# A recurrence that feeds a routed MoE: due times of the static plan taken from a table

## The chip, the cores and the metric

The kernel runs on one core of a Trainium2 chip. The time is the device time of one execution in microseconds (us), a median over runs. The engines are named as the profile names them: PE (matrix unit; PEld its weight loads), DVE (vector), ACT (scalar), POOL (GpSimd), SP (the queue that issues most DMAs).

## The reference, cut to what matters

```python
# 4 sequences of 5056 tokens, 256 channels; 20224 tokens in all
sig = 1 / (1 + exp(-f_logit)); f = lower_bound + (1 - lower_bound) * sig
h[t] = f[:, t] * h[t-1] + (1 - f[:, t]) * x[:, t]     # along each sequence
expert = token_ids * 2654435761 % 8                   # one of 8 experts for each token
out[token] = relu(h[token] @ w1[expert]) @ w2[expert] # w1: 256 x 1024, w2: 1024 x 256
```

The multiplier is 1 modulo 8, so a token's expert is `id & 7`, and the kernel sorts the tokens by that.

## The kernel before, in words

**Stages.** The 5056 steps are cut into 24 blocks of 64, 128 or 256 steps (`TS`), all four sequences together; a block has two to eight *groups* of 128 tokens (158 in all). Blocks 0 to 6 bring the channels onto the partitions with PE transposes (tasks `trf`, `trx`, line 602), take the sigmoid on ACT (`sig`), the gate (`fg`), a product on DVE (`st`), the scan on DVE (`sc`), and go back through PE (`yt`) and a copy (`ye`). Blocks 7 to 23 use DVE's 32x32 transposes instead (`tf`, `tx`, line 783; `yt`, line 843), with the sigmoid of a whole half block on ACT ahead of them (`sig`, line 756). Loads (`ldf`, `ldx`) come from SP; a pool of three pairs of buffers (`XF`) holds them.

**Sort.** Each token's rank within its expert is counted in four ranges of groups (0 to 6, 6 to 46, 46 to 78, 78 to 158): one-hot and running sum (`ra`), PE (`rpe`), `rb`, `rc`, and a split of the rank into tile and row (`rd`). For groups from 46 on, the ids come by `tok` loads, and `ra9` extracts them. `zfd` is a one-element memset on DVE that follows the fill of a stretch of the sorted array `srt` with zeros. POOL then writes each group's rows of h to `srt` by an indirect DMA (`si`, line 537), 158 in all.

**Experts.** An expert's slots are 21 tiles of 128 rows; 168 tiles in all. A tile is read with a DMA transpose from SP (`rd`, line 935), multiplied by w1 (`up`, line 944), relu on ACT (`re`, line 953), multiplied by w2 (`dn`, line 962), copied for two tiles at a time (`oc`, line 970), and its rows go to `out` by an indirect DMA from POOL (`ro`, line 976), 168 in all. Windows say which blocks can reach which tile: tile j may be read when the scatters of block `last[j]` and all before it are out. Tables (`tb`, `tp`, `ta`) find the token of each slot, which `ro` needs. A flag (`flag`, `flagpe`, `flagc`) tells whether a token fell out of its window, for a fallback behind a branch at the end.

**Order.** Nothing is scheduled at run time: each engine works through one list in order. `Plan.order` makes the lists ahead of time. Each task has an engine, an assumed duration, dependencies, buffers and a number, its due time; among tasks that could start within a short look-ahead, the one with the lowest due time goes first. A weight has, besides, an earliest time (`rel`). Block k is due at 6 + 2.3 us for each group before it (`due`), its tables 25 later (`TABD`), its tiles 20 after its end (`OFF`), its rows 8 after its start. The plan's times shape the order only; on the chip engines wait on semaphores. A task at the head of a list that can't start holds back all behind it. On POOL, scatters `si`, rows `ro` and weights `w` share one list; on SP, loads and tile reads do.

Of the kernel before, what the change touches and what calls it, by code (L numbers as in the profile page):

```python
# [1 line left out]

# [6 lines left out]
FP32 = mybir.dt.float32  # L9
# [18 lines left out]
G0 = [sum(NGS[:k]) for k in range(NB)]
# [4 lines left out]
FILL = (9, 12)  # L33
XF = 3
OFF, TABD = 20.0, 25.0
W0, W1 = 8.0, 4.0


def sd(chunks):
# [3 lines left out]
def window(k):  # L43

    a, b = G0[k], G0[k] + NGS[k]
    if a >= MID:
        a, b = NG - b, NG - a
    lo = max(int((16 * a - Z * sd(a)) // P), 0) if a else 0
    hi = int((16 * b + Z * sd(b)) // P)
    return (lo, hi) if G0[k] < MID else (TPE - 1 - hi, TPE - 1 - lo)  # L50


class Task:
# [94 lines left out]
def kernel(  # L148
# [10 lines left out]
    nc = tc.nc  # L159
# [54 lines left out]
    diag = rp.tile([P, 4], FP32, name="diag")  # L214
    diag_i = rp.tile([P, 4], I32, name="diag_i")
    hand = rp.tile([P, 8], FP32, name="hand")
    handt = rp.tile([P, 8, 4], FP32, name="handt")
    row_id = rp.tile([P, NG], I32, name="row_id")
    row_t = rp.tile([P, NG], I32, name="row_t")
# [120 lines left out]
            nc.gpsimd.dma_start(lb_col[:], lower_bound.rearrange("(h p) -> p h", h=2))  # L340

    def load_lbc():
        with nc.allow_non_contiguous_dma(reason="256 values"):
            for b in range(B):
                nc.sync.dma_start(lb_c[32 * b:32 * b + 32, :], lower_bound.rearrange("(c j) -> j c", c=8))

    nz = (FILL[1] - FILL[0]) * D
    zero = rp.tile([P, nz], BF16, name="zero")
# [13 lines left out]
        nc.vector.tensor_scalar(c_col[:], lb_col[:], -1.0, 1.0, op0=ALU.mult, op1=ALU.add)  # L362

    def lbc_dve():
        nc.vector.tensor_scalar(c_c[:], lb_c[:], -1.0, 1.0, op0=ALU.mult, op1=ALU.add)

    lbl = add("lb", {"POOL": 0.9}, -101, load_lb, dma=0.8, lat=2.0)
    ip = add("ip", {"POOL": 4.0}, -100, init_pool)
    ip1 = add("ip1", {"POOL": 2.5}, -99, init_pool1)
    idv = add("idv", {"DVE": 0.2}, -100, init_dve)  # L370
    idv2 = add("idv2", {"DVE": 0.5}, -99, init_dve2, [ip])
    wm = add("wm0", {"DVE": 0.1}, -98, lambda: nc.vector.memset(wrm[:], 0.0))
    add("wm", {"ACT": 1.5}, -98, warm, [wm])
    zf = add("fill", {"SP": 0.5}, -5, fill, [ip1], dma=4.5, lat=2.0)
    ip2 = add("ip2", {"POOL": 4.0}, 0, init_pool2)
    ip3 = add("ip3", {"POOL": 2.0}, 60, init_pool3)
    idv3 = add("idv3", {"DVE": 1.2}, 12, init_dve3, [ip, ip2])
    idv4 = add("idv4", {"DVE": 0.8}, 30, init_dve4, [idv2, ip2])
    lbcl = add("lbcl", {"SP": 1.8}, 20, load_lbc, dma=0.5, lat=2.0)
    lbc = add("lbc", {"DVE": 0.1}, 40, lbc_dve, [lbcl])  # L380
    lbd = add("lbd", {"DVE": 0.1}, -95, lb_dve, [lbl])
    idl = {}
    for k in range(KS):
        idl[k] = add(f"ids{k}", {"ACT" if k < 4 else "POOL": 1.2 if TS[k] > 64 else 1.4},
                     k - 105 if k < 4 else k - 99.5, lambda k=k: load_ids(k), dma=0.6, lat=2.0)
    tokl = [add(f"tok{b}", {"SP": 0.45}, -30, lambda b=b: load_tok(b, 0), dma=0.4, lat=2.0) for b in range(B)]
    if NA % 32:
# [70 lines left out]
        nc.vector.tensor_copy(lo_h[:, a:b], r_i[:])  # L458

    ranked, split = {}, {}  # L460
    zfd = add("zfd", {"DVE": 0.1}, 5, filled, [zf])
    ras = {}
    r0a = add("ra9", {"DVE": 0.8}, 13, rank_0a, tokl + [idv])
    for ri, (a, b) in enumerate(RANGES):
        n = b - a
        pr = (-60, 1, 15, 29)[ri]
        r0 = r0a if a >= GA else add(
            f"ra{a}", {"DVE": 0.4}, pr, lambda a=a, b=b: rank_0(a, b), [idl[k] for k in range(KS) if a <= G0[k] < b]
        )
        ras[a] = add(f"ra{a}", {"DVE": 0.4 + n * 0.028}, pr, lambda a=a, b=b: rank_a(a, b), [r0, idv2, ip1])  # L470
    for ri, (a, b) in enumerate(RANGES):
        n = b - a
        pr = (-60, 1, 15, 29)[ri]
        need = [ras[p] for p, q in RANGES if (q <= b if a < MID else p >= a)]
        rbs = []
        for g in range(2):
            key = ("hp", ("rps", a, g))
            rpe = add(f"rpe{a}{g}", {"PE": 1.0 + n * 0.007}, pr, lambda a=a, b=b, g=g: rank_pe(a, b, g),
                      need + [idv], alloc=key)
            rbs.append(add(f"rb{a}{g}", {"DVE": 0.1 + n * 0.0042}, pr, lambda a=a, b=b, g=g: rank_b(a, b, g),  # L480
                           [rpe], use=[key]))
        rc = add(f"rc{a}", {"DVE": 0.35 + n * 0.013}, pr, lambda a=a, b=b: rank_c(a, b), rbs + ([zfd] if a >= GA else []))
        rd = add(f"rd{a}", {"DVE": 1.4}, 18 + 10 * ri, lambda a=a, b=b: rank_d(a, b), [rc])
        for k in range(NB):
            if a <= G0[k] < b:
                ranked[k], split[k] = rc, rd
# [27 lines left out]
        nc.vector.reduce_max(m[:], v[:], axis=mybir.AxisListType.X)  # L514
        nc.vector.tensor_copy(flag_i[:], m[:])

    mf = add("flag", {"DVE": 0.9}, 150, make_flag, list(set(ranked.values())) + [ip3])
    fp = add("flagpe", {"PE": 0.1}, 151, flag_pe, [mf], alloc=("op", "flag"))
    add("flagc", {"DVE": 0.5}, 152, flag_out, [fp], use=[("op", "flag")])

    weights = []
    for e in range(E):
# [5 lines left out]
                    nc.gpsimd.dma_start(w2_sb[e][:], moe_w2[e].rearrange("(k p) d -> p k d", p=P))  # L528
            weights.append(add(f"w{e}{v}", {"POOL": 0.85}, 5, wl, rel=W0 + W1 * (2 * e + v), dma=2.8, lat=2.0))

    due = {k: 6 + 2.3 * G0[k] for k in range(NB)}
    scat = {}

    prev_y, evs = {}, {}
# [9 lines left out]
    for k in range(KS):  # L544
# [36 lines left out]
        for u in range(nu):  # L581
# [11 lines left out]
            for h in range(2):  # L593
# [32 lines left out]
                def scan(un=un, h=h, bs=bs, k=k, tt=tt):  # L626
# [24 lines left out]
                        use=[ks, kx] + ([kv] if h else []), after=scs)  # L651
                f1 = not T["new", k]
                a = add(
                    f"sc{k}.{u}", {"DVE": nb * 0.06 + cols * 0.00229}, hp_, scan, [a],
                    alloc=ky if f1 else None, use=[ks, kv] + ([] if f1 else [ky]) + ([("y", k - 1)] if k else []),
                    after=scs + ([] if f1 else [T["new", k][0]]),
                )
# [203 lines left out]
    for k in range(NB):  # L861
        jlo, jhi = win[k]
        W = 8 * (jhi - jlo + 1)
        ng = NGS[k]

        def tb(c0, c1, k=k, jlo=jlo, W=W):
            if c0 == 0:
                T["tb", k] = (
                    mp.tile([P, NGM, P], BF16, name="A", bufs=1), mp.tile([P, NGM, 2, WMAX], BF16, name="BP", bufs=1)
                )  # L870
            A, BP = T["tb", k]
            n = c1 - c0
# [37 lines left out]
        pr = due[k] + TABD  # L910
        parts = []
        for c0 in range(0, ng, 4):
            c1 = min(c0 + 4, ng)
            parts.append(add(
                f"tb{k}", {"DVE": 0.4 + (c1 - c0) * (128 + 3 * W) / 960}, pr, lambda c0=c0, c1=c1, f=tb: f(c0, c1),
                [split[k], idv3, evs[k]] + parts[:1], alloc=None if parts else ("tb", k), use=[("tb", k)] if parts else [],
            ))
        b = add(f"tp{k}", {"PE": ng * (0.03 + 2 * W / 2400)}, pr, tpe, parts, alloc=("op", ("tp", k)), use=[("tb", k)])
        tabs[k] = add(f"ta{k}", {"DVE": 0.9}, pr + 0.1, tadd, [b] + ([tabs[k - 1]] if k else []), use=[("op", ("tp", k))])

    seq = sorted((last[j], j, e) for j in range(TPE) for e in range(E))
    for n, (lb, j, e) in enumerate(seq):
        key = lambda p, j=j, e=e: (p, (j, e))
        h = n % 2
# [49 lines left out]
        def rows(j=j, e=e, n=n, h=h):  # L974
# [5 lines left out]
            tc.declare_no_dep(bi.ins, group="rows", reason="the rows of two tiles are disjoint")  # L980
            tc.add_to_no_dep_group("rows", bi.ins)

        rd = add(f"rd{j}.{e}", {"SP": 1.22}, pr, read, [t for k in range(lb + 1) for t in scat[k]],
                 alloc=key("xe"), dma=0.25, lat=2.0)
        u = add(f"up{j}.{e}", {"PE": 0.91}, pr, up, [rd, weights[2 * e]], alloc=key("hp"), use=[key("xe")])
        r = add(f"re{j}.{e}", {"ACT": 1.03, "DVE": 1.18}, -1000 + pr, relu, [u], alloc=key("hT"), use=[key("hp")], alt=True)
# [4 lines left out]
        else:  # L991
            o = add(f"oc{j}.{e}", {"ACT": 0.58, "DVE": 0.62}, -1000 + pr, outc, [d0, d], alloc=ok, use=[pk], alt=True)
            for hh, (jj, ee, ll) in enumerate((first, (j, e, lb))):
                add(f"ro{jj}.{ee}", {"POOL": 1.28}, due[ll] + 8 + 0.01 * n,
                    lambda f=rows, jj=jj, ee=ee, n=n, hh=hh: f(jj, ee, n, hh), [o, tabs[ll]], use=[ok],
                    dma=0.4, lat=2.0)

    order = pl.order()
    for t in order:
        if t.alt:  # L1000
# [103 lines left out]
```

## Time and profile before

| | |
|---|---|
| time, median of 3 runs | 533.04 us (531.91 to 533.26) |
| profiled span | 533.0 us |
| indirect DMAs on POOL | 158 scatters and 168 rows, about 1.03 us each |
| first and last row to `out` | 121.2 us, 522.9 us |
| first `up` matmul | 107.6 us |
| last scatter of block 6, 13, 19, 23 ends | 120.9, 283.6, 454.2, 498.1 us |
| DMA queues | 94.5 MB, mean 177 GB/s |

Busy time is time in which an engine executes; the time between two instructions is put down to what released the second one. For an indirect DMA the busy time is that of POOL, not that of the data's way. "x" is a count. A number in brackets in a timeline is the idle time before the instruction and what ended it.

### The profile page before, as it was taken

To read this page: it belongs to the slowest core of one execution; us is meant where nothing else is said; L and a number is where in the kernel's file an instruction comes from. 1 tells how busy PE (TensorE), PEld (TensorE's weight loads), DVE (VectorE), ACT (ScalarE), POOL (GpSimd) and SP (SyncE) were. 2 spreads that over 40 slices of the span, in tenths; PEclk is the share of its full clock that TensorE was granted. 3 is DMA by queue.
4 is the path that set the end of the run, shared out by engine and by line. 5 is a ranking of instruction groups with operands and counts; after the bars stand their busy time and mean duration, and the time that the engine had idled before them with its cause. 6 is when DMAs were issued, how large, how long until landed. Compare 5 with 4: busy or idle time off the path is not lost. (4 is left out here: it accounts for less than half of the span.)

```text
span 533.0 us, 12517 instructions
## 1 busy us (share of the span) xinstructions
PE 401.2 (75%) x4571; PEld 342.2 (64%) x4571; DVE 344.9 (65%) x799; ACT 353.6 (66%) x534; POOL 359.3 (67%) x426
## 2 busy tenths in 40 slices
PE   4614777696749977986788698787799976499990
PEld 3413555485638766876677587676688865399990
DVE  5928999879758997798498599599488230100000
ACT  5602577778757879694796698776688854167670
POOL 8446345777747777677677577777477767767752
PEclk9756566688977999899699799899799989599996
DMA  8999999278999999898997984936344342245431
GB/s 209 287 281 279 283 282 242 81 203 205 217 237 238 193 207 214 194 219 178 217 207 171 225 179 103 207 111 189 104 126 134 93 119 85 83 113 118 129 93 41
DMA packets 114720, 94.51 MB, mean 177 GB/s; under 512 B 60426, under 2 KB 99902, under 8 KB 114656
## 3 DMA queue, kind: packets, MB, share of 16 engines
q1 hardware_dynamic: 89040, 54.15, 44.8%
q0 software_dynamic: 23744, 39.51, 31.6%
q8 instruction: 37, 0.61, 0.5%
q10 hardware_dynamic: 1872, 0.02, 0.2%
q14 instruction: 27, 0.22, 0.1%
HBM read 58.36 MB, written 33.95 MB: 173 GB/s over the span
## 5 line engine op out<-in xcount | busy, mean ns | idle before, releaser
L976 POOL DMA_INDIRECT out_dram<-ob,row_i x168 | 172.5, 1027 | 75.4 <-issue 37.8
L537 POOL DMA_INDIRECT srt<-yT,pos_i x158 | 162.8, 1030 | 78.0 <-issue 38.4
L962 PE MATMUL op<-w,hT 128*128 128x256 bf16 x1344 | 177.3, 285 | 39.6 <-ACT hT L953 36.8
L953 ACT ACTIVATE hT<-hp 128x1024 bf16<-128x1024 f32 x168 | 164.9, 1020 | 60.3 <-PE hp L944 59.6
L944 PE MATMUL hp<-xe,w 128*128 128x128 bf16 x2688 | 179.2, 228 | 21.1 <-DMA xe<-srt 21.1
L944 PEld LDWEIGHTS <-w 128*128 128x128 bf16 x2688 | 170.0, 103 | 25.4 <-DMA xe<-srt 22.9
L962 PEld LDWEIGHTS <-hT 128*128 128x128 bf16 x1344 | 125.1, 102 | 75.4 <-ACT hT L953 48.4
L826 DVE TENSOR_TENSOR_SCAN y<-sT,y,xT 128x256 bf16<-128x256 f32 (+2 forms) x128 | 77.7, 656 | 1.8
L797 ACT ACTIVATE sT<-sT,lb_c,c_c 128x256 f32<-128x256 f32 (+2 forms) x136 | 70.7, 561 | 4.2 <-DVE sT L783 3.2
L970 ACT COPY ob<-op 128x512 f32<-128x512 f32 x84 | 49.1, 584 | 32.2 <-PE op L962 31.9
L809 DVE SCALAR_TENSOR_TENSOR xT<-sT,xT 128x512 f32<-128x512 f32 x56 | 38.1, 680 | 45.6 <-ACT sT L797 45.0
L843 DVE STREAM_TRANSPOSE yT<-y 128x256 f32<-128x256 f32 (+2 forms) x68 | 24.6, 384 | 43.4 <-DMA srt<-yT,pos_i 30.5
L756 ACT ACTIVATE f_t<-f_t 128x1024 f32<-128x1024 f32 (+1 forms) x29 | 29.3, 1026 | 19.5 <-DMA f_t<-in_f_logit_dram 19.5
L783 DVE STREAM_TRANSPOSE xT<-x_t 128x512 f32<-128x512 f32 (+1 forms) x64 | 38.2, 607 | 2.0 <-DMA x_t<-in_x_dram 2.0
L783 DVE STREAM_TRANSPOSE sT<-f_t 128x512 f32<-128x512 f32 (+1 forms) x64 | 38.5, 613 | 0.3 <-issue 0.2
L686 ACT COPY yT<-yp 128x512 bf16<-128x512 bf16 x23 | 13.4, 583 | 38.0 <-PE tp L892 21.7
L636 DVE TENSOR_TENSOR_SCAN y<-sT,y,xT 128x256 bf16<-128x256 f32 (+1 forms) x48 | 33.6, 706 | 1.5
L899 DVE TENSOR_TENSOR Tab<-Tab,tp 128x48 f32<-128x48 f32 (+4 forms) x24 | 4.6, 191 | 45.4 <-PE tp L892 45.2
L602 PE MATMUL tf<-idf,f_t 128*128 128x128 f32 x92 | 27.1, 401 | 7.4 <-DMA f_t<-in_f_logit_dram 5.9
L602 PE MATMUL tx<-idf,x_t 128*128 128x128 f32 x92 | 26.5, 388 | 6.0 <-ACT yT L686 2.3
L614 ACT ACTIVATE sT<-sT,lb_col,c_col 128x256 f32<-128x256 f32 x46 | 27.6, 601 | 1.1
L875 DVE TENSOR_TENSOR A<-iota_lo,lo_h 128x512 bf16<-128x512 bf16 (+1 forms) x41 | 26.2, 640 | 0.0
(103 smaller groups left out, 231.2 us busy)
## 6 DMA issues: line engine op xcount, KB each, us to landing
f_t<-in_f_logit_dram SPq DMA_DIRECT2D x50, 256.0 KB
x_t<-in_x_dram SPq DMA_DIRECT2D x50, 256.0 KB
w<-in_moe_w_dram POOLq DMA_DIRECT2D x16, 512.0 KB
f_t<-in_f_logit_dram SPq DMA_DIRECT2D x10, 512.0 KB
x_t<-in_x_dram SPq DMA_DIRECT2D x10, 512.0 KB
xe<-srt SPq DMA_TRANSPOSE x168
out_dram<-ob,row_i POOLq DMA_INDIRECT x168
srt<-yT,pos_i POOLq DMA_INDIRECT x158
```

Source lines behind the costliest of these rows:

```text
L537: bi = nc.gpsimd.indirect_dma_start(out=srt[:], out_offset=bass.IndirectOffsetOnAxis(ap=pos_i[:, G0[k] + m:G0[k] + m + 1], axis=0), in_=T[ ...
L602: nc.tensor.transpose(view(t), T[which, k][:, u * nch + n, h * P:(h + 1) * P], idf[:])
L636: nc.vector.tensor_tensor_scan(yv[:, h, b, :tt], T["sT", un][:, c], T["vT", un][:, c], init, op0=ALU.mult, op1=ALU.subtract,)
L783: nc.vector.transpose(o, i_)
L797: nc.scalar.activation(v, v, AF.Identity, scale=c_c[:, c:c + 1], bias=lb_c[:, c:c + 1])
L809: nc.vector.scalar_tensor_tensor(x_.rearrange("p s c l -> p (s c l)"), f_.rearrange("p s c l -> p (s c l)"), 1.0, x_.rearrange("p s c l -> ...
L826: nc.vector.tensor_tensor_scan(yv(T["y", k])[:, cp, :L, s], T["sT", k, u][:, s, n, :], T["xT", k, u][:, s, n, :], init, op0=ALU.mult, op1= ...
L944: nc.tensor.matmul(hp[:, f, :], lhsT=w1_sb[e][:, h, f * P:(f + 1) * P], rhs=xe[:, h, :], start=(h == 0), stop=(h == 1),)
L953: nc.scalar.activation(hT[:], T["hp", j, e][:], AF.Relu)
L962: nc.tensor.matmul(op[:, h, :], lhsT=T["hT", j, e][:, f, :], rhs=w2_sb[e][:, f, :], start=(f == 0), stop=(f == FF - 1),)
L970: nc.scalar.copy(ob[:], T["op", n // 2][:])
L976: bi = nc.gpsimd.indirect_dma_start(out=out, out_offset=bass.IndirectOffsetOnAxis(ap=row_i[:, c:c + 1], axis=0), in_=T["ob", n // 2][:, h, ...
```

## The change

A table `SHIFT` with a number for each block and kind of task is added to the due times: `t` for tile reads, up, relu, down and copies (by the block that the tile waits for), `r` for the rows to `out`, `b` for the tables, `w` for each of the 16 weight loads (to its earliest time), `l` for loads, `s` for scatters, `k` for the work of the recurrence. The numbers were found by a search on a model of the time with noise in it. The ranks of groups from 46 on, until now due at 15 and 29, become due 30 before their first block; `zfd` and `ra9` go with them. The flag is due at 200 instead of 150. The weights start at 14 and follow every 3 instead of 8 and 4. Some assumed durations are set anew. Besides, the lower bound for the later blocks (`lb_c`) is loaded as one row, broadcast to all partitions, then transposed on DVE, instead of by four loads with one value to a descriptor. A tile's read now depends by `last[j]`, which is what it was. `K1` is 0 and leaves the tiles' order as it is.

```diff
-W0, W1 = 8.0, 4.0
+W0, W1 = 14.0, 3.0
+K1 = 0
+SHIFT = {
+    "b": [0.1, 0, 0, 0, 0, -0, -1.1, 0, -5, -1.5, 6.1, 1.5, -1.3, -3.2, -2, -9.7, -1.9, 21.9, 15.3, 23, 15.4, 24.4,
+        0.5, 14.3],
...
+    "r": [0, 0, 0, -0.1, 0, 2.7, -14.4, -25.3, 0, -8.1, -19.7, -15.6, -23.2, 19, 10.1, 10.1, 29, 29, 27.2, 27.2,
+        27.2, 27.2, 0, 8],
+    "s": [0, 12, -3.1, -12.2, -4, -12.3, -16.6, 0.2, 0.6, -11.8, 1.1, -11.2, 13.2, 4.3, -6.6, -6.6, -12.1, -12.1,
+        -16.8, -13.7, -13.7, -14.2, -8.5, -4.7],
...
+    "w": [-6.1, -13.3, 0, 1.7, 3.2, -3.2, 1.1, 1.1, 1.1, -5.5, 3.2, -3.2, 0.5, 3.7, -10.3, 1.2],
+}
+def shift(name, last):
...
+    return SHIFT[kind][last[n] if kind in "tr" else n]
@@ load_lbc
-            for b in range(B):
-                nc.sync.dma_start(lb_c[32 * b:32 * b + 32, :], lower_bound.rearrange("(c j) -> j c", c=8))
+        nc.sync.dma_start(lb_row[:], lower_bound.rearrange("(o d) -> o d", o=1).to_broadcast((P, D)))
@@ lbc_dve
+        nc.vector.transpose(lb_all.rearrange("p c i -> p (c i)"), lb_row[:])
+        nc.vector.tensor_copy(lb_c[:], lb_all[:, :, 0])
...
-    zfd = add("zfd", {"DVE": 0.1}, 5, filled, [zf])
+    rank_pr = [-60, 1] + [due[G0.index(a)] - 30 for a, _ in RANGES[2:]]
+    zfd = add("zfd", {"DVE": 0.1}, rank_pr[2], filled, [zf])
-    r0a = add("ra9", {"DVE": 0.8}, 13, rank_0a, tokl + [idv])
+    r0a = add("ra9", {"DVE": 0.8}, rank_pr[2] - 1, rank_0a, tokl + [idv])
-        pr = (-60, 1, 15, 29)[ri]
+        pr = rank_pr[ri]
...
-        rd = add(f"rd{a}", {"DVE": 1.4}, 18 + 10 * ri, lambda a=a, b=b: rank_d(a, b), [rc])
+        rd = add(f"rd{a}", {"DVE": 1.0}, pr + 20, lambda a=a, b=b: rank_d(a, b), [rc])
...
-    mf = add("flag", {"DVE": 0.9}, 150, make_flag, list(set(ranked.values())) + [ip3])
+    mf = add("flag", {"DVE": 1.4}, 200, make_flag, list(set(ranked.values())) + [ip3])
...
+    for t in pl.tasks:
+        if t.name in WEIGHTS:
+            t.rel = max(t.rel + shift(t.name, last), 0.0)
+        else:
+            t.prio += shift(t.name, last)
     order = pl.order()
```

More of the change, by code (lines that the diff above doesn't have):

```diff
@@ L1 @@
+import re
 from contextlib import ExitStack
@@ L35 @@
 OFF, TABD = 20.0, 25.0
-W0, W1 = 8.0, 4.0
+W0, W1 = 14.0, 3.0
[3 more added lines that the diff above has]
+        0.5, 14.3],
+    "k": [-3.6, -1.4, 0, 0, 0, -1.3, -0.7, -0.7, -0.7, -0.7, -0.7, 8.7, 0.3, 4.1, 7.9, 0, -1.6, -3.2, -1.9, -1.7,
+        -3.3, 7.1, -0.7, -1],
+    "l": [0.9, -1.8, 11.1, -2.3, 2.7, 7.7, -0.5, 1.9, 0, 0, -1.1, 1.2, 0, 2.8, 6.2, 14.9, 6.2, 19.8, 12.1, 9.3, -8.2,
+        0.3, -5.1, -11.2],
+    "r": [0, 0, 0, -0.1, 0, 2.7, -14.4, -25.3, 0, -8.1, -19.7, -15.6, -23.2, 19, 10.1, 10.1, 29, 29, 27.2, 27.2,
+        27.2, 27.2, 0, 8],
+    "s": [0, 12, -3.1, -12.2, -4, -12.3, -16.6, 0.2, 0.6, -11.8, 1.1, -11.2, 13.2, 4.3, -6.6, -6.6, -12.1, -12.1,
+        -16.8, -13.7, -13.7, -14.2, -8.5, -4.7],
+    "t": [0, 0, -1.8, -9.4, 0, 2.6, 4.1, 16.2, 0, 0.1, 4.9, 1.6, 2.8, 2.8, -0.4, 9.2, 9.2, 3.8, 11.4, 3.8, -4.1,
+        -0.5, 0, 2.4],
+    "w": [-6.1, -13.3, 0, 1.7, 3.2, -3.2, 1.1, 1.1, 1.1, -5.5, 3.2, -3.2, 0.5, 3.7, -10.3, 1.2],
+}
+WEIGHTS = [f"w{e}{v}" for e in range(E) for v in range(2)]
 def sd(chunks):
@@ L50, in window @@
     return (lo, hi) if G0[k] < MID else (TPE - 1 - hi, TPE - 1 - lo)
+KIND = {n: kind for kind, names in {
+    "t": "rd up re dn oc", "r": "ro", "b": "tb tp ta", "w": "w", "l": "ldf ldx", "s": "si",
+    "k": "trf trx sig fg st sc yt ye yc tf tx",
+}.items() for n in names.split()}
+def shift(name, last):
+    m = re.fullmatch(r"([a-z]+)(\d+)(\.\d+)?", name)
+    kind = KIND.get(m.group(1)) if m else None
+    if kind is None or m.group(1) == "rd" and not m.group(3):
+        return 0.0
+    n = int(m.group(2))
+    if kind == "w":
+        n = n // 10 * 2 + n % 10
+    return SHIFT[kind][last[n] if kind in "tr" else n]
 class Task:
@@ L216 @@
     hand = rp.tile([P, 8], FP32, name="hand")
+    lb_row = rp.tile([P, D], FP32, name="lb_row")
+    lb_all = rp.tile([P, 8, 32], FP32, name="lb_all")
     handt = rp.tile([P, 8, 4], FP32, name="handt")
@@ L342, in load_lbc @@
     def load_lbc():
-        with nc.allow_non_contiguous_dma(reason="256 values"):
-            for b in range(B):
-                nc.sync.dma_start(lb_c[32 * b:32 * b + 32, :], lower_bound.rearrange("(c j) -> j c", c=8))
+        nc.sync.dma_start(lb_row[:], lower_bound.rearrange("(o d) -> o d", o=1).to_broadcast((P, D)))
     nz = (FILL[1] - FILL[0]) * D
@@ L364, in lbc_dve @@
     def lbc_dve():
+        nc.vector.transpose(lb_all.rearrange("p c i -> p (c i)"), lb_row[:])
+        nc.vector.tensor_copy(lb_c[:], lb_all[:, :, 0])
         nc.vector.tensor_scalar(c_c[:], lb_c[:], -1.0, 1.0, op0=ALU.mult, op1=ALU.add)
+    due = {k: 6 + 2.3 * G0[k] for k in range(NB)}
     lbl = add("lb", {"POOL": 0.9}, -101, load_lb, dma=0.8, lat=2.0)
-    ip = add("ip", {"POOL": 4.0}, -100, init_pool)
-    ip1 = add("ip1", {"POOL": 2.5}, -99, init_pool1)
+    ip = add("ip", {"POOL": 1.4}, -100, init_pool)
+    ip1 = add("ip1", {"POOL": 2.6}, -99, init_pool1)
     idv = add("idv", {"DVE": 0.2}, -100, init_dve)
@@ L374 @@
     zf = add("fill", {"SP": 0.5}, -5, fill, [ip1], dma=4.5, lat=2.0)
-    ip2 = add("ip2", {"POOL": 4.0}, 0, init_pool2)
+    ip2 = add("ip2", {"POOL": 2.6}, 0, init_pool2)
     ip3 = add("ip3", {"POOL": 2.0}, 60, init_pool3)
     idv3 = add("idv3", {"DVE": 1.2}, 12, init_dve3, [ip, ip2])
-    idv4 = add("idv4", {"DVE": 0.8}, 30, init_dve4, [idv2, ip2])
-    lbcl = add("lbcl", {"SP": 1.8}, 20, load_lbc, dma=0.5, lat=2.0)
-    lbc = add("lbc", {"DVE": 0.1}, 40, lbc_dve, [lbcl])
+    idv4 = add("idv4", {"DVE": 0.6}, 60, init_dve4, [idv2, ip2])
+    lbcl = add("lbcl", {"SP": 0.45}, 30, load_lbc, dma=0.5, lat=2.0)
+    lbc = add("lbc", {"DVE": 0.6}, 50, lbc_dve, [lbcl])
     lbd = add("lbd", {"DVE": 0.1}, -95, lb_dve, [lbl])
@@ L383 @@
     for k in range(KS):
-        idl[k] = add(f"ids{k}", {"ACT" if k < 4 else "POOL": 1.2 if TS[k] > 64 else 1.4},
+        idl[k] = add(f"ids{k}", {"ACT" if k < 4 else "POOL": 0.7 if TS[k] > 64 else 1.4},
                      k - 105 if k < 4 else k - 99.5, lambda k=k: load_ids(k), dma=0.6, lat=2.0)
@@ L472 @@
         n = b - a
-        pr = (-60, 1, 15, 29)[ri]
+        pr = rank_pr[ri]
         need = [ras[p] for p, q in RANGES if (q <= b if a < MID else p >= a)]
@@ L515, in flag_out @@
         nc.vector.tensor_copy(flag_i[:], m[:])
-    mf = add("flag", {"DVE": 0.9}, 150, make_flag, list(set(ranked.values())) + [ip3])
-    fp = add("flagpe", {"PE": 0.1}, 151, flag_pe, [mf], alloc=("op", "flag"))
-    add("flagc", {"DVE": 0.5}, 152, flag_out, [fp], use=[("op", "flag")])
+    mf = add("flag", {"DVE": 1.4}, 200, make_flag, list(set(ranked.values())) + [ip3])
+    fp = add("flagpe", {"PE": 0.1}, 201, flag_pe, [mf], alloc=("op", "flag"))
+    add("flagc", {"DVE": 0.7}, 202, flag_out, [fp], use=[("op", "flag")])
     weights = []
@@ L529 @@
             weights.append(add(f"w{e}{v}", {"POOL": 0.85}, 5, wl, rel=W0 + W1 * (2 * e + v), dma=2.8, lat=2.0))
-    due = {k: 6 + 2.3 * G0[k] for k in range(NB)}
     scat = {}
@@ L653 @@
                 a = add(
-                    f"sc{k}.{u}", {"DVE": nb * 0.06 + cols * 0.00229}, hp_, scan, [a],
+                    f"sc{k}.{u}", {"DVE": nb * 0.1 + cols * 0.00254}, hp_, scan, [a],
                     alloc=ky if f1 else None, use=[ks, kv] + ([] if f1 else [ky]) + ([("y", k - 1)] if k else []),
@@ L914 @@
             parts.append(add(
-                f"tb{k}", {"DVE": 0.4 + (c1 - c0) * (128 + 3 * W) / 960}, pr, lambda c0=c0, c1=c1, f=tb: f(c0, c1),
+                f"tb{k}", {"DVE": 0.45 + (c1 - c0) * (128 + 3 * W) / 890}, pr, lambda c0=c0, c1=c1, f=tb: f(c0, c1),
                 [split[k], idv3, evs[k]] + parts[:1], alloc=None if parts else ("tb", k), use=[("tb", k)] if parts else [],
@@ L918 @@
         b = add(f"tp{k}", {"PE": ng * (0.03 + 2 * W / 2400)}, pr, tpe, parts, alloc=("op", ("tp", k)), use=[("tb", k)])
-        tabs[k] = add(f"ta{k}", {"DVE": 0.9}, pr + 0.1, tadd, [b] + ([tabs[k - 1]] if k else []), use=[("op", ("tp", k))])
-    seq = sorted((last[j], j, e) for j in range(TPE) for e in range(E))
+        tabs[k] = add(f"ta{k}", {"DVE": 0.55}, pr + 0.1, tadd, [b] + ([tabs[k - 1]] if k else []), use=[("op", ("tp", k))])
+    seq = sorted(
+        ((max(last[j], K1), j, e) for j in range(TPE) for e in range(E)),
+        key=lambda t: (t[0], t[2] // 2, t[1], t[2]) if t[0] == K1 else (t[0], t[1], t[2]),
+    )
     for n, (lb, j, e) in enumerate(seq):
@@ L981, in rows @@
             tc.add_to_no_dep_group("rows", bi.ins)
-        rd = add(f"rd{j}.{e}", {"SP": 1.22}, pr, read, [t for k in range(lb + 1) for t in scat[k]],
+        rd = add(f"rd{j}.{e}", {"SP": 1.22}, pr, read, [t for k in range(last[j] + 1) for t in scat[k]],
                  alloc=key("xe"), dma=0.25, lat=2.0)
```

## The prediction

> **What bounds the kernel now.** I read the page first: engine shares, the 40 slices, the costliest groups.
>
> ```profile
> PE 401.2 (75%) x4571; PEld 342.2 (64%) x4571; DVE 344.9 (65%) x799; ACT 353.6 (66%) x534; POOL 359.3 (67%) x426
> DMA  8999999278999999898997984936344342245431
> L976 POOL DMA_INDIRECT out_dram<-ob,row_i x168 | 172.5, 1027 | 75.4 <-issue 37.8 <-ACT ob L970 28.6 <-ACT hT L953 5.2
> L537 POOL DMA_INDIRECT srt<-yT,pos_i x158 | 162.8, 1030 | 78.0 <-issue 38.4 <-DMA w<-in_moe_w_dram 22.3 <-DVE yT L843 6.7
> ```
>
> No engine is over 75% by busy time. But POOL's gaps "issue" are 0.30 us ahead of almost every indirect DMA, so each of the 326 row DMAs holds POOL for about 1.03 + 0.30 = 1.33 us. From 89.5 us (in the POOL timeline its last wait for a weight ends there; 24 scatters are done) 302 are left, 402 us of POOL; they end at 524. So POOL is 92% taken from 89.5 us to the last row, with only 434.5 - 402 = 33 us of other idle time. POOL is the bound. In the trace block 19's rows are ready at 371 us and scattered from 427: the recurrence waits for POOL, not the reverse. After the last row 9 us of span remain, which no order changes.
>
> Then stretches (us, then busy us and counts of PE, PEld, DVE, ACT, POOL; granted clock, DMA share, GB/s):
>
> ```profile
> 25.00:46.50 21.50, 2.80 (x65) 2.33 (x64) 10.39 (x28) 1.52 (x4) 10.82 (x58) 0.50 1.23 272
> 46.50:93.00 46.50, 34.71 (x215) 25.17 (x213) 44.44 (x118) 30.35 (x65) 22.00 (x22) 0.61 1.18 275
> 93.00:107.60 14.60, 9.69 (x58) 6.05 (x58) 13.16 (x30) 9.85 (x20) 11.25 (x12) 0.62 0.31 84
> 121.00:384.00 263.00, 208.09 (x2490) 180.00 (x2489) 210.13 (x418) 196.32 (x277) 187.97 (x180) 0.90 0.89 192
> 430.00:461.00 31.00, 16.22 (x191) 13.93 (x189) 3.60 (x19) 10.21 (x12) 22.64 (x24) 0.81 0.30 93
> 475.00:524.00 49.00, 45.46 (x612) 42.58 (x610) 0.51 (x3) 32.83 (x40) 33.34 (x34) 1.00 0.45 112
> ```
>
> Three things stand out. From 25 to 46.5 us PE, ACT and half of DVE stand still. In 121 to 384 POOL idles 263 - 180 x 1.33 = 24 us. PE starves in 430 to 461 (15 us idle) while POOL works, then is full from 475 to the end while POOL idles.
>
> What ends those waits (engine, waited for: us, times, longest; then timelines with the idle time in brackets):
>
> ```profile
> DVE tlow L395 <- DMA tok<-in_moe_token_ids_dram: 6.7, 1, 6.7
> DVE tmp L434 <- issue: 3.9, 1, 3.9
> ```
> ```profile
> 23.13 10.05 SPq L345 DMA_DIRECT2D lb_c<-in_lower_bound_dram  x4
> 33.27 5.42 SPq L560 DMA_DIRECT2D f_t<-in_f_logit_dram  x1
> ```
> ```profile
> 253.03 1.06 ACT L756 ACTIVATE f_t<-f_t 128x1024 f32<-128x1024 f32 x1 [6.57 <-DMA f_t<-in_f_logit_dram]
> 295.34 1.06 ACT L756 ACTIVATE f_t<-f_t 128x1024 f32<-128x1024 f32 x1 [4.56 <-DMA f_t<-in_f_logit_dram]
> 374.60 0.63 ACT L756 ACTIVATE f_t<-f_t 128x512 f32<-128x512 f32 x1 [5.50 <-DMA f_t<-in_f_logit_dram]
> ```
> ```profile
> 504.46 0.98 POOL L976 DMA_INDIRECT out_dram<-ob,row_i  x1 [1.25 <-ACT ob L970]
> ```
>
> The rank of the later tokens (ra9) sits on DVE before its ids have landed; the 3.9 us go to the memset zfd, which waits for the fill of srt. ACT waits at a sigmoid for a load while relus that PE needs stand behind it. The last rows come at PE's pace.
>
> **What the skill says.** "Perfetto Trace Analysis", section "Summary: the profiler window per engine type": for a DMA that GpSimd issues, the window ends with the descriptors, the movement lies after it. The trace agrees: 0.98 us on POOL whatever the load, a few us before a read can follow. So these rows are POOL occupancy, which no order shrinks. "DMA: Bandwidth & Descriptors", section "Rules for kernel authors": a non-contiguous last dimension makes a descriptor per element. It agrees: four loads of 1 KB hold SP for 10.05 us. "TensorE: Matmul & The Clock Gate", section "HAM oscillation": idle PE loses its clock. It agrees: 0.50 in 25 to 46.5, 0.81 in 430 to 461, against 1.00 at the end. Hence a removed PE stall brings some speed too; I price it at nothing.
>
> **The change, part by part.** Instruction counts hardly change; the orders do. Positions below are counted in the two programs' orders.
>
> *Early ranks.* ra9, zfd and the ranks of groups 46 on move behind blocks 4 to 6, where ids and fill have long landed. The two waits, 6.7 + 3.9 = 10.6 us of DVE, go. The rank work itself (some 8 us) still precedes block 7. The flag (4 + 4 small DVE operations, about 2 us) moves to block 13, under POOL's bound: nothing. lb_c becomes one load and a transpose (under 1 us of DVE, by the 0.68 us of a 128x512 transpose), and frees SP for about 9 us just ahead of block 4's loads. Against the gain stands DMA: share 1.16 to 1.23 from 13 to 93 us, where 13 x 205 + 12 x 289 + 21.5 x 272 + 46.5 x 275 give 24.8 MB; loads of blocks 0 to 6 (12.1), weights (8.4), fill (1.6) and scatters of about 40 groups (2.6) are 24.7. The hole let DMA run ahead, and POOL's own waits for weights (22.3 us in 8) remain. Bounds 0 and 10.6; I take 6.
>
> *Weights.* Same 16 DMAs, later start (14, then every 3, with offsets); w10 now follows three scatters. The 48 memsets of ip3 (x 0.13 = 6.3 us) go ahead of the first scatter. Both move POOL work inside the time before 89.5 in which POOL idles some 40 us: nothing, within the bounds just given.
>
> *Middle.* What I count is where a block's sigmoid stands on ACT against where its last load of f and x stands on SP among the tiles' reads. Before, sig16, sig17, sig18 and sig20 stand 4, 4, 6 and 4 tiles ahead of their loads' place; after, 1, 0, 4 and 0. sig12, 13 and 19 also gain 2 each; only sig21 loses 2. The three waits quoted (16.6 us) starve PE and, after that, POOL: its gaps in answer are 2.6 + 1.1 + 0.8, 3.7 and 5.7 = 13.9 us. The largest other POOL gap (6.3 at 150, for DVE's yT of block 9) may go or stay. New orders make new small stalls. Bounds of the gain 3 and 20; I take 12.
>
> *Tail.* Tile 17's first read stands behind 280 row DMAs before and 264 after; its 32 last tiles took from 460.9 to 520 on PE, 59 us, or 46 POOL slots of 1.285. Before: 280 + 46 = 326, exactly the number of row DMAs, so PE sets the end. After: 264 + 46 = 310, and by tile 20 (behind 304, 8 tiles, 11 slots) 315, plus about 4 slots of landing, read and copy: 319. The 24 rows behind the last scatter then run back to back (16 before). POOL's idle time from 384 to 524 us is 140 - 99.5 busy - 102 x 0.30 = 10 us, nearly all of it rows that wait for ob. Bounds 0 and 10; I take 8. Runs of eight scatters hold rows back 8 x 1.285 = 10.3 us; the four ob buffers take 8 tiles, 14 us of PE, so that hides.
>
> *Sum:* 6 + 12 + 8 = 26; 533 - 26 = **507 us**. As a check, POOL without any idle time would end the span at 89.5 - 6 + 402 + 9 = 494.5, so 507 leaves it 12.5 us where 33 were.
>
> **The rivals.** *Full gain:* early 10.6, middle 18, tail 10: 533 - 39 = 494. For it: the hole is idle time; against: the early DMA share. *Small gain:* early 0 because DMA is the bound there, middle 5, tail 8: 520. For it: 24.8 MB against 24.7, and a middle with DVE at 80% and the DMA share at 0.89, so that a wait removed for ACT can come back as one for DVE or a load. *Slower:* the early gain is nothing, the scatter runs of blocks 14 and 18 to 20 find DVE late (tables of 13 and 15 now stand ahead of later blocks) or rows wait behind scatters whose block isn't ready; 7 blocks x 3 us = 21, less 8 from the tail: 546. Against it: block 19 led its scatter by 56 us.
>
> **How the numbers follow.** 507: 0.50; 494: 0.16; 520: 0.22; slower 0.09; within 0.3% by cancelling 0.03. The range reaches from just under the full gain to just over the small one, 492 to 524, and leaves out the slower case and the edges. Faster 0.88, same 0.03, slower 0.09.
>
> **What would show it.** Right: no hole at 25 to 46 us and the first up matmul near 101 instead of 107.6; the ACT waits for f_t under 8 us (19.5); POOL rows back to back after the last scatter; POOL idle without "issue" between first and last row near 13. Wrong: PE's first tile still at 107 (DMA was the bound), POOL waiting for DVE yT in blocks 14 to 20, or new PE waits for xe.

## The result and the profile after

The changed kernel takes **518.26 us** (515.56 to 519.44, four runs), the kernel before 533.15 beside it: ratio 0.9717, 95% interval 0.9676 to 0.9758, so 15 us or 2.8% less. Medians and ranges here and below are over all runs; the ratios leave out single runs in a slower state (one of `e1_early_undone`, several on both sides of `e12_tail_undone`). 507 was forecast, with a range of 492 to 524; the rival "small gain" said 520. The trace of the changed kernel has other line numbers: scatters are L577, rows to `out` L1019, the block sigmoid L796, relu L996.

First the page: engine totals, DMA share in 40 slices, the two groups of indirect DMAs (count, busy us, mean ns, idle before and its cause).

```profile
PE 394.9 (76%) x4571; PEld 336.7 (65%) x4571; DVE 346.4 (67%) x801; ACT 353.5 (68%) x534; POOL 364.3 (70%) x426
DMA  8999999549999998896969979593754534345521
L1019 POOL DMA_INDIRECT out_dram<-ob,row_i x168 | 172.9, 1029 | 61.3 <-issue 38.1
L577 POOL DMA_INDIRECT srt<-yT,pos_i x158 | 167.2, 1058 | 53.2 <-issue 38.9
```

The instructions are the same, but for two small ones on DVE for `lb_c`; the idle time ahead of POOL's row DMAs fell from 75.4 + 78.0 to 61.3 + 53.2 us, of which the 77 us of "issue" belong to the DMAs themselves. DMA is full for as many slices at the start as before.

Now the stretches (us, then busy us and counts of PE, PEld, DVE, ACT, POOL; granted clock, DMA share, GB/s).

```profile
25.00:46.50 21.50, 15.47 (x96) 11.11 (x95) 20.64 (x52) 15.69 (x34) 7.67 (x8) 0.66 1.17 298
46.50:93.00 46.50, 24.51 (x195) 18.91 (x195) 35.96 (x90) 21.75 (x47) 24.47 (x24) 0.61 1.16 258
93.00:107.60 14.60, 7.53 (x65) 5.96 (x64) 14.16 (x34) 9.25 (x18) 11.20 (x12) 0.72 0.42 97
121.00:384.00 263.00, 216.63 (x2634) 186.76 (x2632) 216.71 (x427) 205.29 (x290) 196.32 (x185) 0.93 0.92 196
430.00:461.00 31.00, 30.56 (x420) 28.57 (x418) 2.30 (x14) 19.96 (x24) 23.69 (x25) 1.00 0.43 116
475.00:524.00 49.00, 28.00 (x365) 25.13 (x363) 0.00 (x0) 19.46 (x24) 25.69 (x27) 0.89 0.29 83
```

The hole of 25 to 46.5 us is closed: PE works 15.5 us instead of 2.8, DVE 20.6 instead of 10.4. But in the next stretch *less* gets done: DVE works 36.0 us instead of 44.4, PE 24.5 instead of 34.7. The bytes moved by 93 us are the same: 25 x 247 + 21.5 x 298 + 46.5 x 258 give 24.6 MB, against 24.8. In 430 to 461 PE is now full (it worked 16 of 31 us).

What fills the second stretch: waits between 50 and 100 us (engine, waited for: us, times, longest).

```profile
ACT yT L726 <- DMA srt<-yT,pos_i: 12.3, 1, 12.3
POOL w L567 <- DMA w<-in_moe_w_dram: 7.0, 1, 7.0
POOL w L569 <- DMA w<-in_moe_w_dram: 6.0, 1, 6.0
```

By the profile, POOL stands at a weight load until weights issued before it have landed. The plan has no such dependency, so why POOL has to wait there is not shown. The scatters behind stand too; so the buffers of yT don't come free, ACT's copy waits for a scatter to land, and PE and DVE behind it. The hole has moved, not gone.

And the end, from POOL's timeline (start, us, what, idle before in brackets), from the last scatters to the last row.

```profile
476.77 0.98 POOL L577 DMA_INDIRECT srt<-yT,pos_i  x1 [0.30 <-issue]
478.05 0.98 POOL L1019 DMA_INDIRECT out_dram<-ob,row_i  x1 [0.30 <-DMA srt<-yT,pos_i]
...
507.63 0.98 POOL L1019 DMA_INDIRECT out_dram<-ob,row_i  x1 [0.30 <-issue]
```

24 rows run back to back, 1.286 us each.

As POOL is the bound, I count along its 326 row DMAs in order, and read from each trace when the 46th ends (block 6's last scatter), and how long POOL takes from the 100th to the 240th and from there to the last. The three columns are of one traced execution each; the time is the median of all runs:

| kernel | 46th ends, us | 100th to 240th | 240th to last | time, us |
|---|---|---|---|---|
| before | 120.9 | 204.2 | 120.2 | 533.15 |
| changed | 120.8 | 197.3 | 112.6 | 518.26 |
| early stage undone | 122.0 | 199.0 | 111.2 | 520.33 |
| tail alone | 122.1 | 206.3 | 112.0 | 530.29 |
| before, lb_c alone | 121.9 | 203.6 | 119.6 | 533.55 |
| before, sigmoids late | 122.6 | 190.3 | 119.7 | 522.04 |
| sigmoids and tail | 121.6 | 195.3 | 113.6 | 519.06 |
| changed, weights late | 110.3 | 198.2 | 111.5 | 511.28 |
| old ranks, weights late | 112.0 | 196.2 | 112.8 | 512.50 |
| weights late, two more edits | 110.1 | 193.1 | 111.8 | 512.78 |
| before, three edits | 114.3 | 191.3 | 113.2 | 511.44 |
| before, thin weights | 103.1 | 200.4 | 119.1 | 513.70 |
| changed, thin weights | 96.2 | 198.2 | 111.3 | 495.82 |

The first two rows divide the 15.3 us between the two last rows to `out`: nothing at the 46th (0.8 at the 100th), 6.9 in the middle, 7.6 in the tail.

The same count, split into idle and busy: behind the 46th row DMA, POOL's idle time without the 0.3 us ahead of each DMA fell from 31.7 to 12.6 us, by 19.1. But the 280 DMAs themselves took 291.2 us instead of 287.3, mostly the scatters (1058 ns on average instead of 1030), and that gave 3.9 us back. Two traces of the lists of before differ by 1.8 us in this (287.3 and 289.1), so part of the 3.9 may be chance.

### The profile page after: what moved, and what is told of

Same layout as the page of the kernel before. It is cut to its first block, busy times and chain, and to the rows that moved or that the text cites. A ratio compares the mean times of both kernels' runs of the same rounds, so it can differ in the third digit from the quotient of the medians.

```text
span 517.7 us, 12511 instructions
## 1 busy us (share of the span) xinstructions
PE 394.9 (76%) x4571; PEld 336.7 (65%) x4571; DVE 346.4 (67%) x801; ACT 353.5 (68%) x534; POOL 364.3 (70%) x426
## 2 busy tenths in 40 slices
DMA packets 113776, 94.64 MB, mean 183 GB/s; under 512 B 59354, under 2 KB 98958, under 8 KB 113712
## 4 chain that ended last, share of the span: by engine, by line
DMA 28%; PE 24%; issue 15%; ACT 13%; POOL 10%; DVE 7%; SPq 1%; POOLq 1%; ACTq 0%; DVEq 0%
PE op L1005 15%; DMA srt<-yT,pos_i 14%; DMA xe<-srt 8%; ACT hT L996 8%; PE hp L987 7%; POOL out_dram L1019 6%; POOL srt L577 4%; DMA out_dram<-ob,row_i 4%; ACT ob L1013 2%; DVE y L676 2%; ACT sT L837 1%; DVE xT L661 1%; DMA f_t<-in_f_logit_dram 1%; DVE y L866 1%; DMA x_t<-in_x_dram 1%
## 5 line engine op out<-in xcount | busy, mean ns | idle before, releaser
L1019 POOL DMA_INDIRECT out_dram<-ob,row_i x168 | 172.9, 1029 | 61.3 <-issue 38.1
L577 POOL DMA_INDIRECT srt<-yT,pos_i x158 | 167.2, 1058 | 53.2 <-issue 38.9
L996 ACT ACTIVATE hT<-hp 128x1024 bf16<-128x1024 f32 x168 | 165.4, 1021 | 54.3 <-PE hp L987 50.6
L987 PE MATMUL hp<-xe,w 128*128 128x128 bf16 x2688 | 175.9, 225 | 31.1 <-DMA xe<-srt 30.8
L987 PEld LDWEIGHTS <-w 128*128 128x128 bf16 x2688 | 166.4, 101 | 36.9 <-DMA xe<-srt 30.4
L796 ACT ACTIVATE f_t<-f_t 128x1024 f32<-128x1024 f32 (+1 forms) x29 | 29.4, 1026 | 13.8 <-DMA f_t<-in_f_logit_dram 13.8
L642 PE MATMUL tf<-idf,f_t 128*128 128x128 f32 x92 | 25.4, 376 | 7.4 <-POOL zero L294 6.1
L726 ACT COPY yT<-yp 128x512 bf16<-128x512 bf16 x23 | 13.3, 582 | 24.8 <-DMA srt<-yT,pos_i 12.3
L647 ACT ACTIVATE sT<-tf 128x256 f32<-128x256 f32 x46 | 17.3, 377 | 14.9 <-PE tf L642 14.2
```

What stands on the lines that cost most here:

```text
L577: bi = nc.gpsimd.indirect_dma_start(out=srt[:], out_offset=bass.IndirectOffsetOnAxis(ap=pos_i[:, G0[k] + m:G0[k] + m + 1], axis=0), in_=T[ ...
L642: nc.tensor.transpose(view(t), T[which, k][:, u * nch + n, h * P:(h + 1) * P], idf[:])
L987: nc.tensor.matmul(hp[:, f, :], lhsT=w1_sb[e][:, h, f * P:(f + 1) * P], rhs=xe[:, h, :], start=(h == 0), stop=(h == 1),)
L996: nc.scalar.activation(hT[:], T["hp", j, e][:], AF.Relu)
L1019: bi = nc.gpsimd.indirect_dma_start(out=out, out_offset=bass.IndirectOffsetOnAxis(ap=row_i[:, c:c + 1], axis=0), in_=T["ob", n // 2][:, h, ...
```

## The experiments

In most of them the order of tasks is given outright: `ORDER` lists the tasks in the order of one of the plans, or of two plans joined at one task, or with single tasks moved. All of these have the new load of `lb_c`.

```diff
-    order = pl.order()
+    order = [pl.tasks[i] for i in ORDER]
+    for t, o in zip(order, ON):
+        t.on = ON_NAMES[o]
```

`ON` says for each task which engine runs it, as some tasks may run on either of two.

**Early stage undone** (`e1_early_undone`): the lists of before until `up0.0` is reached, then the changed ones.

> The changed kernel, with the lists of the kernel before up to the first up matmul (blocks 0 to 6, early ranks, weights, first tables), then the lists of the changed one; the new load of lb_c stays. Theory A (the prediction's term): the early stage is worth 6 us, so 518 + 6 = 524. Theory B (the early stage is bound by DMA and by POOL's waits for weights, so closing the hole at 25 us only moves the wait): within 2 us of 518, block 6's last scatter at 121 again, the hole back at 25 to 46 us.

520.33 us (516.14 to 524.63), ratio to before 0.971, interval 0.9641 to 0.9778: within 2.1 us of the changed kernel, and not told apart from it. The hole is back,

```profile
25.00:46.50 21.50, 2.19 (x58) 1.77 (x55) 9.67 (x24) 1.36 (x3) 11.04 (x58) 0.50 1.15 288
```

and the 46th DMA ends at 122.0 instead of 120.8, the 100th at 198.9 instead of 198.7. The interval ends at 522 us, below the 524 of theory A. So the prediction's 6 us for this stage are not there, and the time is theory B's. That the DMA and the weights are the reason is not shown by this run; the next ones are about that.

**Thin weights**, on both kernels (`e3_before_thin`, `e4_after_thin`), to see whether the bytes are the bound. Three quarters of each weight's bytes are not loaded, and the quarter that is loaded is used again in their place, with as many matmuls as before (w1 shown, w2 alike):

```diff
-    w1_sb = [wpool.tile([P, 2, F], BF16, name=f"w1_{e}") for e in range(E)]
+    w1_sb = [wpool.tile([P, 2, F // 4], BF16, name=f"w1_{e}") for e in range(E)]
...
-                nc.gpsimd.dma_start(w1_sb[e][:], moe_w1[e].rearrange("(s h k) f -> k s h f", s=2, h=2))
+                nc.gpsimd.dma_start(w1_sb[e][:], moe_w1[e][:, :F // 4].rearrange("(s h k) f -> k s h f", s=2, h=2))
```

> The kernel before, with each expert's w1 and w2 loads cut to a quarter of their bytes (columns 0 to 255 of w1 and rows 0 to 255 of w2, used again in place of the others): the same 16 loads and matmuls, 2.1 MB instead of 8.4, so some 23 us of DMA at 275 GB/s less in the early stage. Theory B: DMA was the bound there, but here the hole of the ranks still stands: first up matmul from 107.6 to about 100, total 525. Theory A (DVE and the hole are the bound): first up at 105 to 107, total 531.

> The changed kernel with the same quarter of the weights' bytes. Theory B: without the DMA bound the closed hole pays: POOL's waits for weights fall from 28 us to under 8, first up from 104 to 92, block 6's last scatter from 121 to about 108, total 518 - 12 = 506, and the gap to the kernel before with thin weights is larger than 15 us. Rival C: the early stage is bound by POOL or DVE itself: 515 to 518.

513.70 us (ratio 0.9632, 0.9592 to 0.9673) and 495.82 us (0.9298, 0.9251 to 0.9345): the bytes cost 19 and 22 us, more than theory B said (8 and 12). POOL's waits for weights with all bytes, before and changed (us, times, longest):

```profile
POOL srt L537 <- DMA w<-in_moe_w_dram: 22.3, 8, 4.0
POOL w L526 <- DMA w<-in_moe_w_dram: 9.1, 2, 6.0
```
```profile
POOL w L569 <- DMA w<-in_moe_w_dram: 16.1, 3, 6.0
POOL w L567 <- DMA w<-in_moe_w_dram: 11.9, 2, 7.0
POOL srt L577 <- DMA w<-in_moe_w_dram: 4.5, 4, 1.4
```

They sum to 31.4 and 32.5 us: the change moved them, it didn't shorten them. With thin weights, the stretch 46.5 to 93 us of the changed kernel, and POOL's only wait for a weight before 95 us:

```profile
46.50:93.00 46.50, 29.23 (x254) 22.04 (x253) 43.33 (x104) 27.94 (x59) 31.59 (x31) 0.76 0.69 178
```
```profile
POOL srt L577 <- DMA w<-in_moe_w_dram: 0.3, 1, 0.3
```

DVE is as busy as the hole's repair promised (43 of 46.5 us) and the DMA share is 0.69. The 46th DMA now ends 6.9 us earlier in the changed kernel than in the one before (96.2 against 103.1): with the bytes away the early stage is worth the 6 us. The gap between the kernels grew by less, from 14.9 to 17.9 us, as the middle stretch now gains only 2.1 us (200.4 against 198.3) where it gained 6.9. What a part is worth depends on the others.

**lb_c alone** (`e5_lb_alone`): all lists of before.

> All lists of the kernel before, written out, with the changed kernel's load of lb_c alone (one row, broadcast, and a transpose on DVE). Theory B (early stage bound by the bytes of DMA): SP is free some 9 us earlier for block 4's loads, but within 1.5 us of 533. Theory A (those loads are what the early stage waits for): 533 - 4 = 529.

533.55 us, ratio 1.0006 (0.9975 to 1.0038): nothing, though SP is free earlier. It is free by about 5 us earlier and not by 9, as the new load holds it too:

```profile
22.59 5.20 SPq L507 DMA_DIRECT2D lb_row<-in_lower_bound_dram  x1
```

The small pieces of the old loads do show in the count of DMA packets: 1072 packets under 512 bytes are gone (59354 instead of 60426), and the old loads had 1024 elements. But a plain load of f behind them held SP for 5.42 us as well (in the prediction's lines), with the DMA full. So how much of their 10.05 us on SP comes from the small pieces is open. The table above also shows by this run how far two traces of the same lists differ: about 1 us in each stretch.

**Weights late** (`e6_weights_late`): the changed lists, but on POOL w30, w31, w40, w41 each behind every second scatter of block 3, and so on until w71 behind the first of block 6; nothing else is moved.

> The changed kernel's lists with one edit: the weight loads from w30 on stand further back on POOL, the last one behind block 6's first scatter instead of block 4's, in the order of the experts. All bytes are loaded. Theory B: weights and loads of blocks 0 to 6 share the DMA until 93 us and it is half idle from 93 to 121, so moving some 2.5 MB there frees POOL and the loads: block 6's last scatter from 121 to about 112, total 518 - 7 = 511. Rival: tile 0 then waits for its weights and what is won at block 6 is lost at the first rows: 518 to 521.

511.28 us (510.72 to 513.12), ratio 0.9593 (0.9546 to 0.9639): 7 us under the changed kernel, all bytes loaded, and the two intervals don't touch. DMA in 93 to 107.6 us, which was 0.42 busy, is now full, and POOL does 32 instructions in the stretch before instead of 24:

```profile
46.50:93.00 46.50, 27.86 (x226) 21.10 (x224) 43.40 (x104) 27.48 (x59) 32.93 (x32) 0.68 1.05 248
93.00:107.60 14.60, 10.68 (x104) 9.00 (x102) 9.32 (x27) 7.59 (x13) 11.83 (x12) 0.66 1.28 170
```

The 46th DMA ends 10.5 us earlier; 4 of these are given back by the 100th (6.1 earlier there).

**Old ranks, weights late** (`e11_old_ranks_weights_late`): the early stage undone, with the weights at the late places.

> The early stage of the kernel before (early ranks, the hole at 25 us) with the weights at the places of the late version, then the changed kernel's lists. It stands to the 511 us of late weights as the early stage undone (520) stands to the changed kernel (518). Theory B: once the weights are out of the way, the late ranks are worth the 6 us that the prediction gave them: 517, first up matmul near 100 against 92.5. Rival: late weights alone make the gain: 511 to 513.

512.50 us (510.61 to 513.64), ratio 0.9623 (0.9574 to 0.9672). Theory B went too far here: even with the weights late the hole costs 1.2 us, which is nothing by these intervals. The bytes were only moved, and DMA stays full in this kernel as in the one with late weights:

```profile
46.50:93.00 46.50, 31.21 (x196) 21.49 (x194) 44.40 (x117) 30.47 (x65) 32.62 (x32) 0.72 1.03 246
93.00:107.60 14.60, 10.38 (x54) 6.36 (x53) 12.91 (x30) 9.67 (x20) 11.86 (x12) 0.50 1.28 191
```

That fits the thin weights, where the closed hole pays once the bytes are away. The first `up` comes at 107.8 us instead of 92.5, yet the 46th row DMA ends at 112.0 instead of 110.3. It is POOL's progress that counts, not PE's start.

**Sigmoids late on before** (`e7_before_sig_late`): on ACT, sig16 behind the relus re7.1 and re7.5 (from re6.5, oc6.5), sig17 behind re8.3 and re8.5 (from re7.3, oc7.7), sig18's first behind re8.7, sig20 behind re11.5 and re11.7, sig22 behind re13.5. Six of these eight instructions now stand among the relus where the changed kernel has them; sig16's first stands two tiles further back, sig22 ten further forward.

> The lists of the kernel before, with one edit on ACT (and the new load of lb_c): the sigmoids of blocks 16, 17, 18, 20 and 22 stand later, behind the relus of the tiles where the changed kernel has them (some 4 tiles). Theory M (the middle's gain is ACT's waits for those loads): ACT's waits for f_t fall from 19.5 us to under 8, POOL's idle time between 90 and 400 us from 24 to about 14, total 533 - 7 = 526. Rival N: a later sigmoid is made up for by waits of DVE or of the gates behind it, as the whole recurrence then comes later: 531 to 534.

522.04 us (520.89 to 524.59), ratio 0.9812 (0.976 to 0.9864): 11 us from eight moved instructions, more than the changed kernel's whole middle. ACT's waits for these loads, in the order before, changed, here:

```profile
ACT f_t L756 <- DMA f_t<-in_f_logit_dram: 19.5, 6, 6.6
```
```profile
ACT f_t L796 <- DMA f_t<-in_f_logit_dram: 13.8, 5, 4.7
```
```profile
ACT f_t L921 <- DMA f_t<-in_f_logit_dram: 3.8, 2, 2.6
```

POOL's gaps above 0.4 us between 90 and 400 us sum to 23.9, 13.6 and 11.8 us. Theory M holds. In the changed kernel three sigmoids still wait for over 3 us (sig8, sig16, sig18),

```profile
117.64 1.06 ACT L796 ACTIVATE f_t<-f_t 128x1024 f32<-128x1024 f32 x1 [3.87 <-DMA f_t<-in_f_logit_dram]
252.53 1.06 ACT L796 ACTIVATE f_t<-f_t 128x1024 f32<-128x1024 f32 x1 [3.44 <-DMA f_t<-in_f_logit_dram]
294.37 1.06 ACT L796 ACTIVATE f_t<-f_t 128x1024 f32<-128x1024 f32 x1 [4.75 <-DMA f_t<-in_f_logit_dram]
```

and POOL's gap behind sig18 is what it was, before and changed:

```profile
301.85 1.41 POOL L976 DMA_INDIRECT out_dram<-ob,row_i  x1 [3.69 <-ACT ob L970]
```
```profile
300.88 0.98 POOL L1019 DMA_INDIRECT out_dram<-ob,row_i  x1 [3.71 <-ACT ob L1013]
```

**Tail alone** (`e2_tail_alone`), before's lists up to si17.7, then the changed ones; and **sigmoids and tail** (`e8_sig_and_tail`), the same join on the lists with late sigmoids.

> The changed kernel's code, with the lists of the kernel before until block 17's last scatter is planned, then those of the changed one. Theory A: the tail is a part of its own, worth 8 us: 533 - 8 = 525, rows back to back after the last scatter. Rival: the tail pays only when PE and POOL already come earlier from the middle: 530 to 533, with POOL idle between the last rows.

> The kernel before's lists up to block 17's last scatter with the five blocks' sigmoids late on ACT (522 us), then the changed kernel's lists. Theory: sigmoids and tail are separate and add up: 522 - 8 = 514, below the changed kernel's 518. Rival: the tail gains only what it gained alone (4) or nothing, as the sigmoids already brought POOL forward: 518 to 522.

530.29 us (523.88 to 531.08), ratio 0.9898 (0.9822 to 0.9975), so 1.3 to 9.5 us; and 519.06 us (516.62 to 519.17), 3 us less than the late sigmoids alone. Both times are in the rivals' ranges. But POOL is not idle between the last rows, as the first rival said: all 24 run back to back, and the tail's own stretch is short in both, 112.0 and 113.6 us, as in every kernel with the changed tail (111.2 to 113.6), against 119.1 to 120.2 in every kernel with the old one. What was lost stands ahead of it. In the second kernel it is seen: at the join, one sigmoid, sig23, now stands ahead of its load,

```profile
388.23 0.63 ACT L921 ACTIVATE f_t<-f_t 128x512 f32<-128x512 f32 x1 [5.27 <-DMA f_t<-in_f_logit_dram]
```

and POOL waits 3.0 us behind it. In the first, the stretch ahead is 2 to 3 us longer than in two traces of the same lists. There POOL waits 4.7 us at 272 us behind sig17, well before the join, where the trace of before has no such gap; that part can't be told from the spread of the runs.

**Three edits** on before (`e10_three_edits`: late sigmoids, late weights, changed tail, old ranks) and **two more edits** on the late weights (`e9_weights_loads_sig`: sig18 four tiles later; block 8's loads ahead of tile 0's reads on SP).

> The kernel before's lists with the sigmoids late, the weights late from w30 on, and the changed kernel's tail, but with the early ranks where they were. Theory: three parts add up, 514 less what late weights bring while the hole of the ranks stands (0 to 3): 511 to 514. Rival: late weights bring their full 7 without the late ranks too: 507.

> The changed kernel's lists with the weights late (511 us) and two more edits: block 18's two sigmoids stand 4 tiles later on ACT, and block 8's loads stand ahead of tile 0's reads on SP, where SP waited for scatters anyway. Theory: the waits for f_t of 7.4 us (sig18) and 5.3 us (sig8) go, and with them POOL gaps of 6.3 and about 2: 511 - 7 = 504. Rival: POOL waits as long for something else: 509 to 512.

511.44 us (ratio 0.9589, 0.9538 to 0.9641): from 519.06, the late weights bring 7.6 us here too, and the early ranks need not be touched for it. The time is in the theory's range, but its reason is wrong: the late weights bring their full 7 us while the hole stands, and it is the tail that brings less than 8. The other gives 512.78 (509.04 to 514.41; 0.9625, 0.9577 to 0.9673): no gain over 511.28, as the rival said, and just above its range. The stretch from the 100th to the 240th did shorten, to 193.1 us in its trace, but the first `up` went back from 92.5 to 107.5 us; two edits in one kernel, so which spent what isn't settled.

**Tail undone** (`e12_tail_undone`): the changed lists until si17.7, then before's.

> The changed kernel's lists until block 17's last scatter is planned, then the kernel before's: single scatters between pairs of rows, 16 rows behind the last scatter instead of 24. Theory A (the tail is worth 8 us): 518 + 8 = 526, and from the 240th row DMA to the last some 120 us as in the kernel before, against 112.6 in the changed one, with rows waiting for ob again at 1.3 us each at the end. Rival (the 4 us of the tail alone is all of it): 520 to 522.

694.51 us beside 693.33 of the kernel before (ratio 1.0028, 0.9997 to 1.0059): it ran on another chip, on which both take 30% longer, and is no evidence on the tail. So the tail undone was not measured. Two groups of waits from its trace, which the other chips' traces don't have in this size (the first is not there at all):

```profile
ACT hT L1121 <- remote: 129.3, 31, 19.4
POOL out_dram L1144 <- ACT ob L1138: 201.0, 63, 9.1
```

ACT's relu waits 129 us for something that the profile calls only "remote", and POOL waits for ACT. On that chip the changed lists up to block 17 bring nothing; with POOL waiting 201 us for ACT it is not the bound there, which would explain it, but no run tests that.

## Why the prediction was right in kind and too large

- **POOL as the bound: right.** On the chips that run before in 533 us, the time follows the end of POOL's row DMAs in every kernel. Between the first and the last row its idle time without "issue" was forecast near 13 us and is 11.4 (30.5 before). That not all of it came off the time is due to the DMAs' own time: the prediction took 1.03 us for each and 0.98 "whatever the load", but 0.98 is a median, single ones take up to 1.5 us, and the sum grew by 3.9 us. It also counted 24 scatters done at 89.5 us where the trace has 22; that moves its sum by 3 us and no conclusion.
- **Early ranks, 6 us: wrong, 0 to 1** (0.8 us by the 100th row DMA; 2 by the run with the stage undone, not told apart from 0). The failed step is "Bounds 0 and 10.6; I take 6": it priced waits of DVE as if POOL had waited for them. The waits of DVE went as said, yet POOL's idle time up to the 46th row DMA is 59 us before and 58 after, and its waits for weights 31.4 and 32.5. The prediction had both numbers that decide it, 24.8 MB moved and 24.7 needed, and took the middle of two bounds instead of the one that the count supported. With thin weights the step gives 6.9 us at the 46th DMA.
- **Weights, nothing: not seen apart from the ranks, and the missed chance.** The two together came to 0 to 2 us. DMA is 0.31 to 0.42 busy in 93 to 107.6 us in both kernels; moving bytes there is worth 7.
- **Middle, 12 us: the mechanism is shown, the size was 6.9.** Where a sigmoid stands against its load decides POOL's gaps. The mis-sized step is the 13.9 us of gaps, nearly all of which "I take 12" counts as gone. 4.8 us of them are left: 1.1 at 264 us after sig16's wait, and the whole 3.7 behind sig18, which by the prediction's own count still stood 4 tiles ahead of its load. Of the rest, 2.0 us went into longer row DMAs. The count of positions also left blocks out: sig22, whose wait is the third of the three quoted, came back by 6 tiles, while sig8 went ahead by 2 and sig23 by 6. "Only sig21 loses 2" is wrong, and sig8 waits 3.9 us anew. The forecast of under 8 us for ACT's waits failed (13.8). Moving five blocks' sigmoids far enough brings 11.
- **Tail, 8 us: right for its stretch,** 7.6. PE no longer starves in 430 to 461 us and the 24 rows run back to back, as worked out from the positions; POOL's idle time from the 240th row DMA on fell from 9.8 to 1.1 us. ACT's copies now wait 7.9 us for `ob` buffers whose rows have yet to land, but POOL doesn't, so the runs of eight scatters do hide. What the tail adds to the whole time is less sure: joined to the lists of before it brought 3.6 and 3.0 us, and the run that undoes it is missing.
- **Flag and lb_c, nothing: right** for lb_c (1.0006); the flag wasn't tried alone.
- **Slower rival:** block 19's rows were ready at 372.5 us and scattered from 415; DVE's lead stood. One of the prediction's signs of being wrong did appear: PE's waits for tile reads (`xe`) grew from 21.1 to 30.8 us, and the first `up` came at 104.0 instead of 101.
- **The clock:** the prediction set idle PE beside a low clock. Its own table also has 0.61 in 46.5 to 93 us with PE 75% busy, so its three readings alone don't show that idle time is the reason. Nothing was priced on it.

So 6 + 12 + 8 = 26 became 1 + 7 + 8 = 15. The time lies inside the range only because the range was drawn to take in the rival "small gain" (0 + 5 + 8, 520 us), which had the early stage right; the forecast itself was 11 us off.

## What to carry to other kernels

Find the queue whose instructions can't be made fewer, here POOL's row DMAs at 1.3 us each, and measure every reordering by when its n-th instruction ends; here another engine that started 15 us earlier was worth nothing, as that end didn't move. Before giving a removed stall a price, count the bytes that have to be in by the end of its stage and divide by the rate the trace shows: here a full DMA turned the stall into another one. And in static lists look for loads waited for by an instruction that others stand behind: moving eight sigmoids was worth 11 us, where the whole searched table brought 15.

## What was not expected of the hardware

The kernel before takes 533 us on two chips and 693 us on a third, where its runs have a PE clock of 0.80 to 0.84 (0.85 to 0.91 on the other two). The one trace from that chip, of the last experiment, has 129 us of ACT's waits that the profile puts down to "remote" and to no engine or queue of the program. What they are stays open. A time from one chip can't be set beside one from another without the kernel before run there too.
